# Cutting the last weight loads at other rows, and half as many, twice as wide matmuls, at the end of a two-problem attention kernel

## The chip, the core and the metric

The kernel runs on one core of one Trainium2 chip. The metric is the device time of one execution in microseconds. Lower is better. The profile shows one execution of its own; times of views count from the start of that execution's span.

## The reference

Two attention problems, A and B, are computed with one query token each, and their results are concatenated. Both have 32 query heads, 16 key-value heads, head width 128, a cache of 8192 positions and model width 576, in bfloat16. A looks at the last 2048 positions of its cache alone (`W = min(4096, max(256, Sk // 4))`), B at all.

```python
q = (x @ wq).reshape(B, Sq, Hq, Dh)           # 576 -> 32 * 128
scores = einsum("bhqd,bhkd->bhqk", q, k) * (Dh ** -0.5)
p = softmax(scores, axis=-1)
o = einsum("bhqk,bhkd->bhqd", p, v)
return o.reshape(B, Sq, Hq * Dh) @ wo         # 4096 -> 576
```

The last line is the output projection: a row of 4096 numbers times `wo`, a matrix of 4096 x 576 (4.6 MB). The two results of 576 numbers each stand side by side in the output.

## The kernel before

**Program.** The kernel records every step with `add(engine, ...)` and the names of what it reads and writes; `Program` derives the semaphore waits from these names. Each engine runs its own steps in the order in which they were recorded. There is no scheduler: the order is written out by hand.

**Attention.** The work is done in five groups: group 0 holds the whole of A, groups 1 to 4 hold four key-value heads of B each. Keys and values come in through four slots of SBUF (`slots`, 16384 elements a partition each): two for keys, two for values. In a group TensorE transposes the keys (L464), multiplies them with the queries (L485), and, after the softmax, multiplies the probabilities with the values (L538). VectorE and ScalarE bring the transposed keys from PSUM back to SBUF.

**Loads.** All large loads are issued by SP, on one queue, in the order of the text. A load waits, at its issue, for the work that last read its part of `slots`. After the values of the last group there stand five loads of `wo` (`load_wo`, issued on L391):

- all 32 rows of A's `wo`, into the key slots, as soon as the keys of the last group are transposed;
- 24 rows of B's `wo`, into the rest of the key slots;
- 5 rows of B's, then 2, then 1, into the first value slot, as soon as that was read.

A "row" here is one of the 32 rows that each of the 128 partitions holds: partition p holds the 32 rows of `wo` from 32p on, each of 576 numbers, so a row is 128 x 576 numbers or 144 KB over all partitions.

**Output projection.** `combine` and `o_columns` (L621) leave the attention's result of each problem in `opj`, one column per row of `wo`. `wo_part` then multiplies, row by row: a row's 576 columns are cut into four pieces of 144, and each piece goes through its own strip of 32 columns of TensorE's array, into its own 32 partitions of a PSUM bank (L634). Only the first partition of each strip holds the result; the others are padding. All 32 rows add up in the bank. `wo_part` runs over A's 32 rows first, then over B's in the pieces in which they were loaded, each piece waiting for its own load:

```python
for P in range(2):
    for Q, lo, n, off, res in wo_loads:
        if Q == P:
            wo_part(P, lo, n, off, res)
    finish_out(P)
```

`finish_out` copies the bank to SBUF on VectorE (L640) and lets SP write the 576 numbers out (L646). The program ends when both outputs have landed. A's projection runs while B's loads are still coming in, B's stands at the very end.

Of the kernel before, what the change touches and what calls it, by code (L numbers as in the profile page):

```python
# [4 lines left out]
BF16 = mybir.dt.bfloat16  # L5
# [5 lines left out]
HQ = 32  # L11
HKV = 16
DH = 128
DM = 576
SK = 8192
SCALE = DH ** -0.5
SLOT = 16384
# [1 line left out]
NG = 5  # L19
NKT = 4  # L20
WQ_W = 18432
OUTW = DM // 4


class Op:
# [11 lines left out]
class Program:  # L37
# [15 lines left out]
    def add(self, eng, fn, reads=(), writes=(), dma=None, after=(), tag=None, inc=1, loop=None):  # L53
        op = Op(eng, fn, tuple(reads), tuple(writes), dma, tag, inc if dma is None or inc > 1 else 16, loop)
        deps = []
        for r in op.reads:
            w = self.writer.get(r)
            if w is not None:
                deps.append((w, True))
            if r[0] == "bank":  # L60
                deps += [(o, False) for o in self.readers.get(r, ())]
        for r in after:
            deps += [(o, False) for o in self.readers.get(r, ())]
        for r in op.writes:
            w = self.writer.get(r)
            if w is not None:
                deps.append((w, False))
            deps += [(o, False) for o in self.readers.get(r, ())]
        for r in op.reads:
            self.readers.setdefault(r, []).append(op)  # L70
        for r in op.writes:
            self.writer[r] = op
            self.readers[r] = []
        for o, raw in deps:
            if o is op:
                continue
            if o.dma is None and o.eng == eng and (not raw or eng in ("pe", "sp")):
                continue
            op.deps.append(o)
            o.needed = True  # L80
        op.order = len(self.ops)
        self.ops.append(op)
        return op
# [192 lines left out]
def bass_concat_heads__sliding_block_cached__gqa_block_cached__decode_kernel(  # L276
# [26 lines left out]
    add = prog.add  # L303

    slots = nc.alloc_sbuf_tensor("slots", [128, 4 * SLOT], BF16)
# [21 lines left out]
    acc = nc.alloc_sbuf_tensor("acc", [128, NG, DH], F32)  # L327
    accs = nc.alloc_sbuf_tensor("accs", [128, NG, DH], F32)
    opj = nc.alloc_sbuf_tensor("opj", [128, 2, 64], BF16)
    outsb = nc.alloc_sbuf_tensor("outsb", [128, 2, OUTW], BF16)  # L330
    warm = nc.alloc_sbuf_tensor("warm", [128, 8], F32)

    ktps = [nc.alloc_psum_tensor("ktps%d" % b, [128, 512], F32) for b in range(4)]
# [291 lines left out]
    def load_wo(P, lo, n, off, res):  # L625
        load(slots[:, off:off + n * DM], lambda: wos[P].rearrange("(p j) n -> p (j n)", p=128)[:, lo * DM:(lo + n) * DM],
             res, "wo%d_%d" % (P, lo))

    def wo_part(P, lo, n, off, res):
        def mm(pe):  # L630
            for jj in range(lo, lo + n):
                for j in range(4):
                    o = off + (jj - lo) * DM + j * OUTW
                    ins = pe.matmul(ktps[P][32 * j:32 * j + 32, 0:OUTW], lhsT=opj[:, P, jj:jj + 32],  # L634
                                    rhs=slots[:, o:o + OUTW], start=(jj == 0), stop=(jj == HQ - 1))
            return ins
        add("pe", mm, reads=[("opj", P)] + res, writes=[("bank", P)])

    def finish_out(P):
        add("dve", lambda dve: dve.tensor_copy(outsb[:, P, :], ktps[P][:, 0:OUTW]), reads=[("bank", P)],  # L640
            writes=[("outsb", P)])

        def put(eng):
            src = bass.AP(tensor=outsb, offset=P * OUTW, ap=[[32 * 2 * OUTW, 4], [1, OUTW]])
            dst = out[0, 0:1, P * DM:(P + 1) * DM].rearrange("o (j n) -> (o j) n", j=4)
            return eng.dma_start(dst, src)  # L646
        add("sp", put, reads=[("outsb", P)], writes=[("out", P)], dma="out%d" % P)

# [2 lines left out]
    for P in range(2):  # L651
        off, res = WQ[P]
# [9 lines left out]
        reads=["sameB0"], writes=["sameB"])  # L662
    sums(pickB[:, :, :], pick[:, :, :].rearrange("p r (i c) -> p r c i", i=4), ["pick"], ["pickB"])

    for g in range(NG):
# [30 lines left out]

    wo_loads = [
        (0, 0, 32, 0, [("k", 0), ("k", 1, 0)]),
        (1, 0, 24, WQ_W, [("k", 1, 1)]),
        (1, 24, 5, 2 * SLOT, [("v", 0, 0), ("v", 0, 1)]),  # L700
        (1, 29, 2, 2 * SLOT + 5 * DM, [("w", 0)]),
        (1, 31, 1, 2 * SLOT + 7 * DM, [("w", 1)])]
    for k, (P, lo, n, off, res) in enumerate(wo_loads):
        if res[0][0] == "w":
            wo_loads[k] = (P, lo, n, off, res)
        load_wo(P, lo, n, off, res)
    combine([NG - 1])
    o_columns(1)
# [5 lines that stand above are left out]
    prog.emit()  # L714
    for P in range(2):
        o = prog.writer[("out", P)]
# [28 lines left out]
```

## Time and profile before

| | us |
|---|---|
| median of 5 runs | 248.68 (248.33 to 248.77) |
| profiled execution | 248.85 |
| its span, first to last instruction | 247.2 |
| TensorE busy | 161.8 (65%) |
| DMA engines busy with the large loads' queue | 97.6% of the span |
| read from memory | 102.76 MB, 416 GB/s over the span |
| granted TensorE clock, mean | 0.827 |

PE is TensorE's matmuls, PEld its weight loads (which overlap matmuls), DVE is VectorE, ACT ScalarE, SP the engine that issues the loads; a q behind an engine's name marks its sequencer. L634 is line 634 of the kernel. A group of instructions is written `out<-in`, with its count behind an x. A matmul `ktps<-slots,opj 128*32 128x144` contracts over 128 partitions, with 32 columns of weights (`opj`) and 144 columns streamed (`slots`). Each matmul comes with a weight load. A matmul's duration is longer than the step from one matmul to the next, since they are pipelined. The granted clock is the share of full speed at which TensorE was allowed to run: in these traces 1.00 or 0.50.

### The profile page before, as it was taken

The page shows a single profiled execution, that of the slowest core. Times are in us where ns is not written, and L with a number is a line of the kernel's source. Part 1 is how long each engine was busy: PE and PEld are TensorE (multiplying, and loading weights), DVE is VectorE, ACT ScalarE, POOL GpSimd, SP SyncE. Part 2 cuts the span into 40 slices and gives each one's busy share as a digit, 9 for nine tenths or more (in the row PEclk, how much of TensorE's full clock was granted, in tenths as well). Part 3 has the DMA queues.
Part 4 walks back from the last instruction along what each step waited for, and adds up shares of the span by engine and source line. Part 5 has one row for each costly group of instructions (what it writes and reads, how often), then busy time and mean ns, then how long its engine had stood idle before and what let it go on. Part 6 is the DMA issues. An engine that isn't in the chain of part 4 may idle for free. (4 is left out here: it accounts for less than half of the span.)

```text
span 247.2 us, 5330 instructions
## 1 busy us (share of the span) xinstructions
PE 161.8 (65%) x2348; PEld 116.5 (47%) x2348; DVE 84.9 (34%) x172; ACT 87.4 (35%) x95; POOL 10.7 (4%) x48
## 2 busy tenths in 40 slices
PE   0014639994706999443999380999581799769716
PEld 0001239782306876213887130977340777435516
DVE  0010124654221465240556331355422255524200
ACT  2000016874003786101778200578500387610000
POOL 7400000000000000000000000000000000000000
PEclk9999577999775999795899766599979599965786
DMA  9998999999999999999999999999999999999991
GB/s 358 406 424 372 424 424 422 422 422 419 468 423 419 430 430 435 430 435 445 431 430 430 435 424 430 424 440 424 435 445 430 430 435 435 424 445 412 433 389 67
DMA packets 5929, 102.89 MB, mean 416 GB/s; under 512 B 928, under 2 KB 1056, under 8 KB 1312
## 3 DMA queue, kind: packets, MB, share of 16 engines
q1 hardware_dynamic: 5632, 102.77, 97.6%
q8 instruction: 6, 0.10, 0.2%
q10 hardware_dynamic: 288, 0.00, 0.1%
q14 instruction: 3, 0.02, 0.0%
HBM read 102.76 MB, written 0.00 MB: 416 GB/s over the span
## 5 line engine op out<-in xcount | busy, mean ns | idle before, releaser
L470 ACT ACTIVATE kt<-ktps 128x1024 bf16<-128x1024 bf16 x80 | 78.5, 1021 | 92.1 <-PE ktps L464 92.1
L464 PE MATMUL ktps<-ident,slots 128*128 128x128 bf16 x1280 | 89.2, 236 | 32.7 <-PEq L214 32.7
L464 PEld LDWEIGHTS ktps<-ident,slots 128*128 128x128 bf16 x1280 | 83.4, 107 | 47.9 <-issue 47.9
L473 DVE COPY kt<-ktps 128x1024 bf16<-128x1024 bf16 x80 | 55.3, 692 | 77.0 <-PE ktps L464 77.0
L538 PE MATMUL opsum<-slots,ptm 128*32 128x512 bf16 x320 | 29.4, 525 | 5.9 <-PEq L214 5.9
L485 PE MATMUL sacc<-kt,qst 128*32 128x512 bf16 x320 | 25.4, 393 | 1.9 <-PEq L214 1.9
L425 PE MATMUL opsum<-slots,xpad 128*32 128x512 bf16 x72 | 7.3, 586 | 22.3 <-DVE xpad L416 22.3
L538 PEld LDWEIGHTS opsum<-slots,ptm 128*32 128x32 bf16 x320 | 12.0, 123 | 18.6 <-issue 15.9
L425 PEld LDWEIGHTS opsum<-slots,xpad 128*32 128x32 bf16 x72 | 2.8, 137 | 25.6 <-issue 25.5
L555 DVE SCALAR_TENSOR_TENSOR acc<-opsum,maskV,acc 128x128 f32<-128x128 f32 x28 | 9.8, 351 | 4.5 <-PE opsum L538 3.7
L516 PE MATMUL misc<-ident,psb 128*128 128x128 bf16 x40 | 3.3, 231 | 11.6 <-PEq L214 11.6
L431 ACT ACTIVATE qrow<-opsum 128x512 bf16<-128x512 f32 x2 | 1.2, 597 | 26.4 <-PE opsum L425 26.4
L454 POOL COPY qst<-qcol 128x8 bf16<-128x8 bf16 x20 | 3.1, 190 | 164.5 <-PE sacc L485 152.1
L634 PE MATMUL ktps<-slots,opj 128*32 128x144 bf16 x256 | 6.3, 276 | 5.1 <-DMA slots<-in_B_wo_dram 5.1
L516 PEld LDWEIGHTS misc<-ident,psb 128*128 128x128 bf16 x40 | 2.5, 102 | 14.0 <-issue 14.0
L506 ACT ACTIVATE psb<-sacc,stat 128x1024 bf16<-128x1024 f32 x5 | 5.6, 1113 | 9.5 <-DVE stat L500 9.5
L485 PEld LDWEIGHTS sacc<-kt,qst 128*32 128x32 bf16 x320 | 5.0, 94 | 7.9 <-issue 4.3
L634 PEld LDWEIGHTS ktps<-slots,opj 128*32 128x32 bf16 x256 | 5.8, 122 | 5.3 <-DMA slots<-in_B_wo_dram 5.3
L525 DVE TENSOR_SCALAR ptm<-misc,par 128x512 bf16<-128x512 bf16 x10 | 4.4, 480 | 10.4 <-PE misc L516 10.4
L416 DVE TENSOR_SCALAR xpad<-xtwo,par 128x5 bf16<-128x5 bf16 (+1 forms) x8 | 1.3, 230 | 16.5 <-DMA xtwo<-in_A_x_dram 12.8
L552 DVE TENSOR_SCALAR acc<-opsum,maskV 128x128 f32<-128x128 f32 x4 | 1.4, 351 | 14.1 <-PE opsum L538 14.1
L498 DVE TENSOR_REDUCE stat<-sacc 128x1 f32<-128x512 f32 x5 | 3.5, 691 | 4.5 <-PE sacc L485 4.5
(62 smaller groups left out, 34.5 us busy)
## 6 DMA issues: line engine op xcount, KB each, us to landing
slots<-in_B_k_cache_dram SPq DMA_DIRECT2D x8, 4096.0 KB
slots<-in_B_v_cache_dram SPq DMA_DIRECT2D x8, 4096.0 KB
slots<-in_A_k_cache_dram SPq DMA_DIRECT2D x8, 1024.0 KB
slots<-in_A_v_cache_dram SPq DMA_DIRECT2D x8, 1024.0 KB
slots<-in_A_wq_dram SPq DMA_DIRECT2D x1, 4608.0 KB, 13.8
slots<-in_B_wq_dram SPq DMA_DIRECT2D x1, 4608.0 KB, 24.5
slots<-in_A_wo_dram SPq DMA_DIRECT2D x1, 4608.0 KB, 19.2
slots<-in_B_wo_dram SPq DMA_DIRECT2D x1, 3456.0 KB, 27.0
```

The costliest lines, as they stand in the source:

```text
L425: ins = pe.matmul(opsum[32 * j:32 * j + 32, P * 512:(P + 1) * 512], lhsT=xpad[:, P, u, :], rhs=slots[:, o:o + 512], start=(u == 0), stop=( ...
L464: ins = pe.matmul(ktps_bf[q][:, t * 128:(t + 1) * 128], lhsT=slots[:, o:o + 128], rhs=ident[:, :], start=True, stop=True, is_transpose=True)
L470: add("act", lambda act, q=q, dst=dst: act.activation(dst, ktps_bf[q], ACT.Copy), reads=[("bank", q)], writes=[("kt", u % NKT, q)], tag="e ...
L473: add("dve", lambda dve, q=q, dst=dst: dve.tensor_copy(dst, ktps_bf[q]), reads=[("bank", q)], writes=[("kt", u % NKT, q)], tag="e%d%d" % ( ...
L485: ins = pe.matmul(sacc[32 * j:32 * j + 32, :], lhsT=qst[:, o:o + 32], rhs=rhs, start=(u == 0 and e == 0), stop=True, skip_group_check=True)
L498: add("dve", lambda dve: dve.tensor_reduce(st(C_M + g), sacc[:, :], AX.X, ALU.max), reads=[B_S], writes=[("st", C_M + g)], tag="max")
L506: return act.activation(psb[:, :].rearrange("p (x g) -> p x g", g=2), src, ACT.Exp, bias=st(C_NB + g), scale=SCALE, accum_out=st(C_L + g))
L516: ins = pe.matmul(dst[:, t * 128:(t + 1) * 128], lhsT=psb[:, t * 128:(t + 1) * 128], rhs=ident[:, :], start=True, stop=True, is_transpose= ...
L525: ins = dve.tensor_scalar(to, src, par2[:, e:e + 1], None, ALU.mult)
L538: ins = pe.matmul(opsum[32 * j:32 * j + 32, s * 512:(s + 1) * 512], lhsT=ptm[:, o:o + 32], rhs=v[:, :, b:b + 128], start=(tt == 0), stop=( ...
L555: add("dve", lambda dve, w=w, src=src: dve.scalar_tensor_tensor(dst, src, w, dst, ALU.mult, ALU.add), reads=[B_O[s], "wlast" if last else ...
L634: ins = pe.matmul(ktps[P][32 * j:32 * j + 32, 0:OUTW], lhsT=opj[:, P, jj:jj + 32], rhs=slots[:, o:o + OUTW], start=(jj == 0), stop=(jj == ...
```

## The change

Two things change. A's output projection takes two matmuls of 288 columns per row, through two strips, for four of 144: 64 matmuls for 128, and with their weight loads 128 instructions fewer in TensorE's program. A's copy to SBUF takes 64 partitions x 288 for 128 x 144, and A's output is written as two pieces of 288 numbers for four of 144. B's projection keeps its four matmuls of 144 columns per row. And B's `wo` comes in loads of 21, 7, 3 and 1 rows for 24, 5, 2 and 1; the number of loads, their order and what each waits for at its issue stay, and `wo_part` waits for B's rows in the new pieces. In the changed kernel the matmul's line is 635 for 634, the copy's 643 for 640, the output's 649 for 646.

```diff
-OUTW = DM // 4
+OUTS = [2, 4]
...
-    outsb = nc.alloc_sbuf_tensor("outsb", [128, 2, OUTW], BF16)
+    outsb = nc.alloc_sbuf_tensor("outsb", [128, 2, DM // 2], BF16)
...
             for jj in range(lo, lo + n):
-                for j in range(4):
-                    o = off + (jj - lo) * DM + j * OUTW
-                    ins = pe.matmul(ktps[P][32 * j:32 * j + 32, 0:OUTW], lhsT=opj[:, P, jj:jj + 32],
-                                    rhs=slots[:, o:o + OUTW], start=(jj == 0), stop=(jj == HQ - 1))
+                w = DM // OUTS[P]
+                for j in range(OUTS[P]):
+                    o = off + (jj - lo) * DM + j * w
+                    ins = pe.matmul(ktps[P][32 * j:32 * j + 32, 0:w], lhsT=opj[:, P, jj:jj + 32],
+                                    rhs=slots[:, o:o + w], start=(jj == 0), stop=(jj == HQ - 1))
...
     def finish_out(P):
-        add("dve", lambda dve: dve.tensor_copy(outsb[:, P, :], ktps[P][:, 0:OUTW]), reads=[("bank", P)],
-            writes=[("outsb", P)])
+        n = OUTS[P]
+        add("dve", lambda dve: dve.tensor_copy(outsb[0:32 * n, P, 0:DM // n], ktps[P][0:32 * n, 0:DM // n]),
+            reads=[("bank", P)], writes=[("outsb", P)])
         def put(eng):
-            src = bass.AP(tensor=outsb, offset=P * OUTW, ap=[[32 * 2 * OUTW, 4], [1, OUTW]])
-            dst = out[0, 0:1, P * DM:(P + 1) * DM].rearrange("o (j n) -> (o j) n", j=4)
+            src = bass.AP(tensor=outsb, offset=P * DM // 2, ap=[[32 * DM, n], [1, DM // n]])
+            dst = out[0, 0:1, P * DM:(P + 1) * DM].rearrange("o (j n) -> (o j) n", j=n)
             return eng.dma_start(dst, src)
...
         (0, 0, 32, 0, [("k", 0), ("k", 1, 0)]),
-        (1, 0, 24, WQ_W, [("k", 1, 1)]),
-        (1, 24, 5, 2 * SLOT, [("v", 0, 0), ("v", 0, 1)]),
-        (1, 29, 2, 2 * SLOT + 5 * DM, [("w", 0)]),
-        (1, 31, 1, 2 * SLOT + 7 * DM, [("w", 1)])]
+        (1, 0, 21, WQ_W, [("k", 1, 1)]),
+        (1, 21, 7, 2 * SLOT, [("v", 0, 0), ("v", 0, 1)]),
+        (1, 28, 3, 2 * SLOT + 7 * DM, [("w", 0)]),
+        (1, 31, 1, 2 * SLOT + 10 * DM, [("w", 1)])]
```

More of the change, by code (lines that the diff above doesn't have):

```diff
@@ L698, in bass_concat_heads__sliding_block_cached__gqa_block_cached__decode_kernel @@
         (0, 0, 32, 0, [("k", 0), ("k", 1, 0)]),
-        (1, 0, 24, WQ_W, [("k", 1, 1)]),
-        (1, 24, 5, 2 * SLOT, [("v", 0, 0), ("v", 0, 1)]),
-        (1, 29, 2, 2 * SLOT + 5 * DM, [("w", 0)]),
-        (1, 31, 1, 2 * SLOT + 7 * DM, [("w", 1)])]
-    for k, (P, lo, n, off, res) in enumerate(wo_loads):
-        if res[0][0] == "w":
-            wo_loads[k] = (P, lo, n, off, res)
+        (1, 0, 21, WQ_W, [("k", 1, 1)]),
+        (1, 21, 7, 2 * SLOT, [("v", 0, 0), ("v", 0, 1)]),
+        (1, 28, 3, 2 * SLOT + 7 * DM, [("w", 0)]),
+        (1, 31, 1, 2 * SLOT + 10 * DM, [("w", 1)])]
+    for P, lo, n, off, res in wo_loads:
         load_wo(P, lo, n, off, res)
```

## The prediction

> **What bounds the kernel now.** I read the page's numbers first: the DMA engines are busy 97.6% of the span with the one load queue, TensorE 65%, so up to the last loads the kernel lasts as long as its 102.8 MB. The change touches only what follows the last attention group, so the chain that ended last, the landings and the clock there come next. The end of the chain (start, duration, what):
>
> ```profile
> 214.02 27.05 DMA slots<-in_B_wo_dram
> 241.06 0.04 issue
> 241.11 4.06 PE ktps L634 x112
> 245.17 0.02 issue
> 245.19 0.31 DVE outsb L640
> ```
>
> The span ends at 247.2. TensorE waits until 241.07 for B's first 24 rows, multiplies all 32 rows in one go until 245.14, then come a copy and the output's DMA, which the change leaves alone for B. The question is what holds the 4.06 us. The four loads of B, with the time from issue to landing, and when SP issued three of them (two in the first line, one in the second):
>
> ```profile
> slots<-in_B_wo_dram SPq DMA_DIRECT2D x1, 3456.0 KB, 27.0
> slots<-in_B_wo_dram SPq DMA_DIRECT2D x1, 720.0 KB, 18.2
> slots<-in_B_wo_dram SPq DMA_DIRECT2D x1, 288.0 KB, 18.5
> slots<-in_B_wo_dram SPq DMA_DIRECT2D x1, 144.0 KB, 18.4
> ```
>
> ```profile
> 224.63 0.80 SPq L391 DMA_DIRECT2D slots<-in_B_wo_dram  x2
> 225.48 0.43 SPq L391 DMA_DIRECT2D slots<-in_B_wo_dram  x1
> ```
>
> The 24 rows land at 214.02+27.05 = 241.07, the 5 at 224.63+18.2 = 242.83, the 2 (issued at 225.00, where the first line's second issue begins) at 243.50, the last row at 225.48+18.4 = 243.88. From 241.07 to 243.88 eight rows land in 2.81 us: 0.35 us a row (0.35 over the 5, 0.34 over the 2, 0.38 for the last). All data is there 1.26 us before TensorE ends, so the end is set by TensorE, which starts late and runs slowly. How slowly, the stretches show (us, length, PE busy and count, PEld, DVE, ACT, POOL, then granted clock, DMA share, GB/s):
>
> ```profile
> 231.90:233.70 1.80, 0.12 (x4) 0.13 (x5) 1.40 (x4) 0.00 (x0) 0.00 (x0) 1.00 1.07 461
> 233.70:236.10 2.40, 2.31 (x136) 2.12 (x135) 0.24 (x2) 0.00 (x0) 0.00 (x0) 1.00 0.96 415
> 236.10:238.50 2.40, 0.00 (x0) 0.00 (x0) 0.26 (x1) 0.00 (x0) 0.00 (x0) 1.00 0.94 401
> 238.50:241.10 2.60, 0.00 (x0) 0.00 (x0) 0.00 (x0) 0.00 (x0) 0.00 (x0) 0.51 0.92 369
> 241.10:245.20 4.10, 4.03 (x128) 3.74 (x128) 0.01 (x1) 0.00 (x0) 0.00 (x0) 0.50 0.24 90
> ```
>
> A's 128 matmuls ran at clock 1.00, B's 128 at 0.50: the clock fell at about 238.5, 2.5 us after A's last matmul ended. The timeline gives the rates:
>
> ```profile
> 235.79 0.23 PE L634 MATMUL ktps<-slots,opj 128*32 128x144 bf16 x1
> 236.39 9.68 SPq L646 DMA_DIRECT2D out_dram<-outsb  x2
> 241.11 4.03 PE L634 MATMUL ktps<-slots,opj 128*32 128x144 bf16 x128 [5.09 <-DMA slots<-in_B_wo_dram]
> ```
>
> A's matmuls start from 233.73 to 235.79: 2.06 us over 127 steps, 16.2 ns each, 65 ns for a row of four. B's last matmul takes 0.32 us, so its 127 steps fill 4.03-0.32 = 3.71 us: 29.2 ns each, 117 ns a row.
>
> **The change, part by part.**
>
> *The first load, 21 rows for 24.* The bytes ahead of the last of those rows shrink by three rows, and the queue never empties, so it lands between 241.07 (no gain) and 241.07-3×0.35 = 240.02. I take 240.02: the three later landings kept the pace of 0.35 us a row whatever the size of the load. TensorE then starts at 240.06 (0.04 after landing, as before).
>
> *The later loads, 7, 3 and 1 rows for 5, 2 and 1.* After them 28, 31 and 32 rows are there; 31 and 32 are the old cuts, so these land at 243.50 and 243.88 as before, and 28 rows at 242.83-0.35 = 242.48. The number of loads and SP's issues and waits stay; the second load waits for the same V slot, the two small ones for nothing.
>
> *A's matmuls, 64 of 288 columns for 128 of 144.* Each row streams the same 576 columns through two 32-column strips of the array, not four. No row of this trace shows two strips beside each other. If issue alone set the pace, 64×16.2 ns = 1.0 us; if nothing ran beside anything, four times 65 ns a row, 8.3 us. I take twice the four-strip price, 130 ns a row, because the columns in each strip double: 4.2 us, so A ends at 233.73+4.2+0.2 = 238.1 for 236.0. That is covered by the wait for B's load until 240.06; the cover ends when A takes over 6.3 us.
>
> The Trainium skill speaks against this part: "TensorE: Matmul & The Clock Gate", Part 3 (packing small matmuls), says that matmuls in different strips run at once and that more strips give more. Its isolated gap of N/2.4+2.5 ns would be 122.5 ns for 288 columns; 64 in a row, none overlapped, would be an estimated 7.8 us, with the end then near the late case below.
>
> *B's matmuls* are unchanged, but each load's rows now wait for their own landing. At half clock: 21 rows from 240.06 to 242.52, 7 rows to 243.34, 3 rows from 243.54 to 243.89, the last from 243.92; its four matmuls end 3×0.029+0.32 = 0.41 later, at 244.33, for 245.14: 0.81 saved. At full clock: 241.43, then 7 rows from 242.52 to 242.98, 3 from 243.54 to 243.74, the last from 243.92 to 243.92+3×0.016+0.23 = 244.20: 0.94 saved. So the clock decides little here; the last landing decides.
>
> Which clock? A's later end shortens the idle time from 5.1 us to 240.06-238.1 = 2.0 us. An idle stretch of about 1.6 us (232.0 to 233.6) kept 1.00, one of 2.5 us lost it: 2.0 lies between, nearer the one that kept it, so full clock is likelier.
>
> The same page, Part 1 (the clock gate), says that the gate falls to half after an idle window of about 3.4 us, free-running against the kernel. Here it fell after 2.5 us of idleness, so a bare rule of 3.4 us of gap isn't what this trace shows; by the page the new gap would keep the clock, and the sum would be the 0.94 above.
>
> If A alone is late (8.3 us, end at 242.3), B follows at full clock: 32 rows × 65 ns = 2.1, plus 0.2 for the last, end 244.65, still 0.5 saved.
>
> *A's copy and output.* The copy takes 64x288 for 128x144, between its old 0.31 and 0.62 us, from 238.1; the issue of A's output moves from 236.39 to about 238.6. Behind it on SP stands only B's output at 245.2 at the earliest today, 244.3 then, over 5 us later. Cost nothing; the wait for the copy that ends last on SP stays B's.
>
> *Code.* TensorE's program loses 64 matmuls and 64 weight loads. The code queue moves:
>
> ```profile
> q8 instruction: 6, 0.10, 0.2%
> ```
>
> about 16.4 KB apiece; one of the six lies after 240 us. At 416/16 = 26 GB/s an engine, one costs its DMA engine 0.63 us. If a fetch goes away from the engine that ends last, up to 0.63 is gained; if one moves onto it, 0.63 is lost. I take 0: the four landings keep their even pace, so neither late fetch seems to sit on that engine.
>
> **Sum.** Against the profiled execution (248.85 us for a span of 247.2, 1.65 around it): 0.81 to 0.94 off the end of TensorE, after which nothing changes (copy 0.31, output 1.7). I take 0.85: 248.0. The median of the runs, 248.68, is 0.17 under the profiled execution, so 247.83 there; I state 247.9, since runs in which the clock returned before B's end have a little less to gain.
>
> **The rivals.**
>
> 1. *The landing doesn't move.* If 21 rows land when 24 did (241.07) and the clock is half, B ends at 245.14: 248.7. The even 0.35 us a row speaks against it, and at full clock the end would still be bounded by 243.88. Chance 0.08.
> 2. *A code fetch falls on the engine that lands last.* The last landing goes from 243.88 to 244.5, the gain to 0.2: 248.5. For: the program's shift by 128 instructions moves the fetch among B's matmuls. Against: the last fetch came too late to matter before, and moves towards the program's end. Chance 0.10.
> 3. *Slower: the clock falls during A.* If two strips count as too little work, A runs at half clock: a row takes 2×117 = 234 ns if pairs overlap, 4×117 = 468 if nothing does; say 300, nearer the pairs. A then ends at 233.73+32×0.3+0.3 = 243.6, B from there at half clock at 243.6+31×0.117+0.41 = 247.65, 2.5 later: 251.2. It decides once A ends after 241.05 with B at half clock (an A row of over 220 ns). Against: B's 32 rows at half clock brought the clock back to 1.00 by 245.5, and A's work is longer than today's. Chance 0.06.
>
> **The numbers.** Forecast 0.76, by itself 247.6 to 248.2 (0.81 to 0.94 with the runs' own scatter of 0.4). The range of 247.4 to 248.5 takes in a vanished code fetch below and rival 2 above; rivals 1 and 3 stay outside. A measurement of this kernel tells about 0.2% (0.5 us) from no change: under 248.2 is faster, over 249.2 slower. Faster: 0.76 and a share of rival 2, 0.80; within: the rest of 2 and 1, 0.14; slower: 0.06.
>
> **What would show it.** Right: B's first matmul near 240.1, A's last near 238, TensorE idle twice or more among B's rows before landings, the last row's matmuls right behind a landing near 243.9, the chain ending in the load of one row instead of 24. Wrong steps would show as: a first matmul still at 241.1 (landing), A's matmuls running past 240 (strips), B's matmuls back to back to 245 (start or clock), a last landing past 244.3 (code or load shape). The forecast as a whole fails if TensorE's last matmul ends after 244.7.

## The result, and the profile after

| | before | after |
|---|---|---|
| median, us | 248.54 (49 runs, 247.66 to 249.24) | 247.88 (28 runs, 247.34 to 248.81) |
| profiled execution, us | 248.85 | 247.49 |
| its span, us | 247.2 | 245.8 |
| code queue | 6 transfers | 5 transfers |

The ratio is 0.9977, with a 95% interval of 0.9969 to 0.9985: 0.57 us (0.37 to 0.77) off 248.54. The kernel became faster: the interval leaves out no change, though the gain is a quarter of a per cent. The later sets of runs gave 1.12 and 0.80 us (below).

The end of the chain in the profiled execution after the change (start, duration, what):

```profile
224.08 18.99 DMA slots<-in_B_wo_dram
243.07 0.04 issue
243.12 0.37 PE ktps L635 x12
243.49 0.00 issue
243.49 0.28 PE ktps L635 x4
243.76 0.02 issue
243.79 0.31 DVE outsb L643
```

Before, the chain's last transfer was the 24-row load and 4.06 us of matmuls stood behind it. Now its last transfer is a small load, and what stands behind it is the last three rows and the last row. The landings and the issues by SP:

```profile
slots<-in_B_wo_dram SPq DMA_DIRECT2D x1, 3024.0 KB, 26.9
slots<-in_B_wo_dram SPq DMA_DIRECT2D x1, 1008.0 KB, 18.4
slots<-in_B_wo_dram SPq DMA_DIRECT2D x1, 432.0 KB, 19.0
slots<-in_B_wo_dram SPq DMA_DIRECT2D x1, 144.0 KB, 18.9
```

```profile
212.73 12.26 SPq L391 DMA_DIRECT2D slots<-in_B_wo_dram  x4
223.71 0.80 SPq L391 DMA_DIRECT2D slots<-in_B_wo_dram  x2
224.56 0.43 SPq L391 DMA_DIRECT2D slots<-in_B_wo_dram  x1
```

21 rows land at 212.73+26.9 = 239.63, 28 at 223.71+18.4 = 242.11, 31 at 224.08+19.0 = 243.08, all 32 at 224.56+18.9 = 243.46. TensorE's side, in the timeline (the bracket is the idle time before and what ended it):

```profile
239.64 1.50 PE L635 MATMUL ktps<-slots,opj 128*32 128x144 bf16 x84 [0.95 <-DMA slots<-in_B_wo_dram]
242.17 0.62 PE L635 MATMUL ktps<-slots,opj 128*32 128x144 bf16 x28 [1.03 <-DMA slots<-in_B_wo_dram]
243.12 0.62 PE L635 MATMUL ktps<-slots,opj 128*32 128x144 bf16 x16 [0.33 <-DMA slots<-in_B_wo_dram]
243.49 0.10 PEld L635 LDWEIGHTS ktps<-slots,opj 128*32 128x32 bf16 x4 [0.19 <-DMA slots<-in_B_wo_dram]
```

TensorE now waits for every one of the four landings, and ends at 243.74, 0.28 us after the last one. Before, it ended 1.26 us after it (245.14 to 243.88). The stretches, with clock, DMA share and GB/s at the end of each row, show at what clock:

```profile
232.90:236.30 3.40, 3.40 (x38) 2.24 (x38) 0.19 (x1) 0.00 (x0) 0.00 (x0) 0.50 1.01 434
236.30:238.70 2.40, 2.39 (x38) 1.69 (x34) 0.00 (x0) 0.00 (x0) 0.00 (x0) 0.99 0.86 366
238.70:239.60 0.90, 0.00 (x0) 0.00 (x0) 0.45 (x1) 0.00 (x0) 0.00 (x0) 1.00 0.92 384
239.60:241.20 1.60, 1.50 (x84) 1.31 (x84) 0.00 (x0) 0.00 (x0) 0.00 (x0) 1.00 0.98 385
241.20:243.80 2.60, 1.24 (x44) 0.72 (x44) 0.01 (x1) 0.00 (x0) 0.00 (x0) 1.00 0.27 100
```

A's 64 matmuls ran at 0.50 for 3.4 us, and the clock came back to 1.00 before they were done; B ran at 1.00 throughout. The code queue, which brings TensorE's program (a transfer on it is called a code fetch below), had five transfers:

```profile
q8 instruction: 5, 0.08, 0.1%
```

### The profile page after: what moved, and what is told of

Same layout as the page of the kernel before. It is cut to its first block, busy times and chain, and to the rows that moved or that the text cites. A ratio compares the mean times of both kernels' runs of the same rounds, so it can differ in the third digit from the quotient of the medians.

```text
span 245.8 us, 5202 instructions
## 1 busy us (share of the span) xinstructions
PE 164.7 (67%) x2284; PEld 115.1 (47%) x2284; DVE 85.0 (35%) x172; ACT 87.1 (35%) x95; POOL 10.8 (4%) x48
## 5 line engine op out<-in xcount | busy, mean ns | idle before, releaser
L464 PE MATMUL ktps<-ident,slots 128*128 128x128 bf16 x1280 | 86.5, 232 | 32.4 <-PEq L214 32.4
L464 PEld LDWEIGHTS ktps<-ident,slots 128*128 128x128 bf16 x1280 | 80.7, 105 | 47.7 <-issue 47.7
L538 PE MATMUL opsum<-slots,ptm 128*32 128x512 bf16 x320 | 31.0, 548 | 5.4 <-PEq L214 5.4
L425 PE MATMUL opsum<-slots,xpad 128*32 128x512 bf16 x72 | 8.1, 630 | 21.5 <-DVE xpad L416 21.5
L516 PE MATMUL misc<-ident,psb 128*128 128x128 bf16 x40 | 4.4, 276 | 11.6 <-PEq L214 11.6
L635 PE MATMUL ktps<-slots,opj 128*32 128x144 bf16 (+1 forms) x192 | 8.5, 270 | 2.3 <-DMA slots<-in_B_wo_dram 2.3
L516 PEld LDWEIGHTS misc<-ident,psb 128*128 128x128 bf16 x40 | 3.3, 122 | 14.0 <-issue 14.0
## 6 DMA issues: line engine op xcount, KB each, us to landing
slots<-in_B_wo_dram SPq DMA_DIRECT2D x1, 3024.0 KB, 26.9
```

The source lines that it names most:

```text
L425: ins = pe.matmul(opsum[32 * j:32 * j + 32, P * 512:(P + 1) * 512], lhsT=xpad[:, P, u, :], rhs=slots[:, o:o + 512], start=(u == 0), stop=( ...
L464: ins = pe.matmul(ktps_bf[q][:, t * 128:(t + 1) * 128], lhsT=slots[:, o:o + 128], rhs=ident[:, :], start=True, stop=True, is_transpose=True)
L516: ins = pe.matmul(dst[:, t * 128:(t + 1) * 128], lhsT=psb[:, t * 128:(t + 1) * 128], rhs=ident[:, :], start=True, stop=True, is_transpose= ...
L538: ins = pe.matmul(opsum[32 * j:32 * j + 32, s * 512:(s + 1) * 512], lhsT=ptm[:, o:o + 32], rhs=v[:, :, b:b + 128], start=(tt == 0), stop=( ...
L635: ins = pe.matmul(ktps[P][32 * j:32 * j + 32, 0:w], lhsT=opj[:, P, jj:jj + 32], rhs=slots[:, o:o + w], start=(jj == 0), stop=(jj == HQ - 1))
```

## The experiments

Theory L: the last landing is a floor for TensorE's end, and B's matmuls reach it either by starting earlier (the cut) or by running at full clock (what fills the idle time before B), so one of the two is enough. Against it stood: only the clock counts (C), only the cut counts (S), the two gains add up, or the shorter program is what helps.

All times below are against the kernel before, run beside it on the same chip. For the gain in us the ratio is applied to the median of the kernel before in the same set of runs. The sets e1 to e4, e5 to e8 and e9 to e12 each ran on a chip of their own.

| run | ratio, interval | us | last landing | TensorE ends | between |
|---|---|---|---|---|---|
| before, first profile | | | 243.88 | 245.14 | 1.26 |
| e5 before, again | 1.0000 (0.9986 to 1.0014) | 0.0 | 244.01 | 245.25 | 1.24 |
| e1 cut only | 0.9980 (0.9963 to 0.9997) | -0.50 | 244.04 | 244.34 | 0.30 |
| e9 cut only, again | 0.9966 (0.9948 to 0.9985) | -0.85 | 243.79 | 244.20 | 0.41 |
| e2 strips only | 0.9968 (0.9955 to 0.9981) | -0.80 | 243.89 | 244.22 | 0.33 |
| e10 strips only, again | 0.9975 (0.9950 to 1.0001) | -0.62 | 243.67 | 244.03 | 0.36 |
| e6 filler of 48 matmuls | 0.9964 (0.9946 to 0.9983) | -0.89 | 244.19 | 244.51 | 0.32 |
| e4 whole change | 0.9955 (0.9942 to 0.9968) | -1.12 | 243.43 | 243.69 | 0.26 |
| e11 whole change, again | 0.9968 (0.9948 to 0.9988) | -0.80 | 243.56 | 243.83 | 0.27 |
| e3 filler of 128 matmuls | 1.0024 (1.0007 to 1.0041) | +0.60 | 243.56 | 245.64 | 2.08 |
| e7 last row first | 1.0128 (1.0108 to 1.0147) | +3.18 | 243.83 | 247.90 | 4.07 |
| e8 pad of 64 | 0.9994 (0.9979 to 1.0009) | -0.15 | 244.13 | 244.42 | 0.29 |
| e12 pad of 256 | 1.0022 (0.9996 to 1.0047) | +0.55 | 244.82 | 245.11 | 0.29 |

The last three columns come from one profiled execution of each: the last load's issue and its time to landing, and the end of the last matmul. The views give the time to landing to 0.1 us, so the last column is good to about 0.05. They show two things apart: the landing, which wanders from execution to execution, and what TensorE adds to it.

**The cut alone (e1, e9).**

```diff
-OUTS = [2, 4]
+OUTS = [4, 4]          # the changed kernel, A back in four strips
```

> Only the loads of 21, 7, 3 and 1 rows; A keeps four strips of 144 columns and the program its length. Theory L (the last landing bounds the end; an earlier start and a full clock are each enough to get there): B starts about 1.0 us before where it starts with 24 rows, still at clock 0.50, and its last row starts within 0.1 us of the last landing; TensorE ends about 0.4 us after that landing, the time is 0.5 to 0.8 us under the kernel before. Rival C (only the clock counts, the cut does nothing): same as before within 0.2 us. Rival S (only the cut counts): the whole gain of the change, the same time as the changed kernel within 0.1 us.

> The cut alone once more (loads of 21, 7, 3 and 1 rows, A in four strips), beside the other part and the whole change on one chip, for narrower intervals. Theory L (each part is enough): 0.6 to 1.0 us under the kernel before, within 0.3 us of the whole change; TensorE ends 0.3 to 0.4 us after the last landing. Theory of separate gains: 0.3 to 0.5 us under before and as far above the whole change.

In e1 B's matmuls start at 240.25 and run at half clock nearly to the end, as in the kernel before:

```profile
240.20:243.70 3.50, 3.45 (x112) 3.26 (x112) 0.00 (x0) 0.00 (x0) 0.00 (x0) 0.51 0.56 221
243.70:244.40 0.70, 0.64 (x20) 0.29 (x16) 0.01 (x1) 0.00 (x0) 0.00 (x0) 1.00 0.00 0
```

Yet they end 0.30 us behind the last landing, where the kernel before needs 1.24 to 1.26: an earlier start alone reaches the floor (the last rows ran at 1.00 here). So rival C is wrong. In e9 the last rows ran at 0.50 and the end came 0.41 after the landing, the price that the prediction had for half clock.

**The strips alone (e2, e10).**

```diff
-        (1, 0, 21, WQ_W, [("k", 1, 1)]),
-        (1, 21, 7, 2 * SLOT, [("v", 0, 0), ("v", 0, 1)]),
-        (1, 28, 3, 2 * SLOT + 7 * DM, [("w", 0)]),
-        (1, 31, 1, 2 * SLOT + 10 * DM, [("w", 1)])]
+        (1, 0, 24, WQ_W, [("k", 1, 1)]),
+        (1, 24, 5, 2 * SLOT, [("v", 0, 0), ("v", 0, 1)]),
+        (1, 29, 2, 2 * SLOT + 5 * DM, [("w", 0)]),
+        (1, 31, 1, 2 * SLOT + 7 * DM, [("w", 1)])]
```

> Only A's 64 matmuls of 288 columns in two strips (128 instructions fewer); B's loads stay at 24, 5, 2 and 1 rows. Theory L: B starts when 24 rows have landed (about 241), at clock 1.00, does these 24 rows in 1.6 us and waits for each later landing; TensorE ends 0.3 us after the last landing, 0.6 to 0.9 us under the kernel before, and within 0.2 us of the changed kernel. Rival C: the same. Rival S: no gain, TensorE busy without a break from 241 on.

> A in two strips alone once more (loads of 24, 5, 2 and 1 rows). Theory L: 0.6 to 1.0 us under before, within 0.3 us of the whole change. Theory of separate gains: as for the cut alone, and both differences add up to that of the whole change.

In e2 B starts at 241.14, as late as in the kernel before, but at full clock:

```profile
238.30:241.10 2.80, 0.00 (x0) 0.00 (x0) 0.45 (x1) 0.00 (x0) 0.00 (x0) 1.00 0.93 372
241.10:242.40 1.30, 1.26 (x80) 1.26 (x84) 0.00 (x0) 0.00 (x0) 0.00 (x0) 0.99 0.48 182
242.40:244.30 1.90, 1.82 (x60) 1.24 (x48) 0.03 (x1) 0.00 (x0) 0.00 (x0) 0.50 0.13 38
```

80 of the 128 matmuls have begun by 242.4, when the clock falls; B then goes on without a break, which the expectation had otherwise, and the end comes 0.33 us behind the landing. So rival S is wrong too.

That the clock holds for 2.8 us of idleness here, but fell 2.5 us after A in the kernel before, shows that the length of the gap alone doesn't decide. The clock records show more: in all fourteen profiles the clock changes only at points that lie whole multiples of 3.41 us apart, and these points fall at other times in each execution. In the kernel before, TensorE was busy for 0.89 us of the stretch from 235.12 to 238.53, and the clock fell at its end. In e2 the idle time is spread over two such stretches: 235.54 to 238.95 (busy 2.73 us, clock kept) and 238.95 to 242.37 (busy 1.23 us, clock lost). So how long B keeps the full clock depends in part on where these points happen to fall. How much work a stretch needs isn't settled: in e10 1.37 us kept the clock in one stretch and lost it in the next.

**The whole change beside its parts (e4, e11).** The kernel is the changed one.

> The changed kernel itself, on the same chip as the parts. Theory L: 0.6 to 0.9 us under the kernel before, no more than 0.2 us under the better of the two parts, and far from the sum of both. Theory of two separate gains: the sum of what the two parts give.

> The whole change once more, beside its parts. Theory L: 0.7 to 1.0 us under before and no more than 0.3 us under the better part. Theory of separate gains: the sum of the parts.

e4 missed its expectation: 0.32 us under the better part rather than 0.2, and not far from the sum of the two (1.30). In the second set, on another chip, the cut gave 0.85, the strips 0.62 and both 0.80, where two separate gains would have given 1.47. The intervals are too wide for the times alone to decide (e11's goes from 0.30 to 1.29 us). The profiles say more: the six kernels end 0.26 to 0.41 us after their landings, against 1.24 to 1.26 before. Either part alone takes away nearly all of that distance, and the other adds at most 0.15 us to it.

The landing is another matter. In the three profiles of the changed kernel the last landing came at 243.43 to 243.56, in the four of its parts at 243.67 to 244.04. The difference is there already when A's `wo` lands (232.4 to 232.5 for 232.7 to 233.0), before the first instruction in which these kernels differ has run. So it is no work of the cut or of the strips as theory L has them; whether these three executions happened to land early, or something else about the program makes them, stays open.

**Fillers in place of the strips (e3, e6).** A's strips stay at four, the loads at 24, 5, 2 and 1; matmuls whose result isn't read go between A and B.

```diff
+            for jj in range(HQ):                 # e3: A's 128 matmuls of 144 columns again, into bank 2
...
+            for t in range(12):                  # e6: 4 * 12 matmuls of 512 columns, into bank 2
...
```

> The kernel before, with A's 128 matmuls in four strips done a second time into an unused PSUM bank (the result isn't read), so that TensorE is idle for about 3 us less before B; loads of 24, 5, 2 and 1 rows; the program is 256 instructions longer. Theory L with the clock as the means: B starts at clock 1.00 or comes to it early, and the time is 0.4 to 0.9 us under the kernel before, though nothing useful was taken away. If it is the shorter program (fewer code fetches) that makes strips faster: no gain here, or 0.2 to 0.6 us slower. Rival S: no gain.

> The kernel before, with 48 matmuls of 512 columns in four strips into an unused PSUM bank between A and B (96 instructions for the 256 of the first filler; the result isn't read). A's own part, the loads and B stay as before. Theory L with the clock as means: no break for code, B starts with its 24 rows' landing at clock 1.00 or comes to it before its end, waits for the later landings, and TensorE ends 0.3 to 0.4 us after the last one: 0.5 to 0.9 us under the kernel before. Rival (the strips help by something other than TensorE's work in the gap, fewer instructions for example): no gain.

e3 went the other way, and the chain says why:

```profile
237.24 0.88 PE ktps L644 x56
238.12 2.74 issue
240.86 2.34 PE ktps L644 x69
243.20 2.45 PE ktps L634 x128
```

After 59 of the filler's 128 matmuls TensorE stood still for 2.74 us with no semaphore to wait for. In just that stretch, 238.2 to 240.8, the code queue moved one block:

```profile
q8 instruction: 1, 0.02, 2.6%
```

By its record this transfer ended at 239.51, and the matmuls went on at 240.86, 1.35 us later. In e12 (below) the same happens among the small matmuls at the start: TensorE stood from 9.69 to 12.46, again with no semaphore to wait for, a block came in from 10.17 to 11.11, and matmuls went on 1.35 us after it. So TensorE had most likely run out of fetched code both times, though no record names that wait. B's first matmul in e3 then came at 242.88, 2.1 us after its 24 rows had landed (213.04+27.7 = 240.74). So e3 tells nothing of the clock, and its loss of 0.60, which the expectation gave for a program's length as the cause, is explained by this stop. e6 fills the time with 96 instructions instead of 256, and there the filler runs without a break and the gain is there:

```profile
236.50:239.20 2.70, 2.70 (x60) 1.10 (x48) 0.31 (x1) 0.00 (x0) 0.00 (x0) 1.00 0.90 377
239.20:241.40 2.20, 0.04 (x7) 0.01 (x4) 0.00 (x0) 0.00 (x0) 0.00 (x0) 1.00 0.90 359
241.40:244.50 3.10, 3.10 (x128) 2.33 (x128) 0.00 (x0) 0.00 (x0) 0.00 (x0) 0.71 0.29 111
```

0.89 us faster, with work added and none taken away, and with B starting at clock 1.00. What helps is the work in the time before B, by way of the clock, and not a shorter program. The two strips fill that time because they are slow, not because they are fewer.

**The kernel before against itself (e5).** No edit.

> The kernel before against itself, as a control and for a second look at its end. All theories: the same within 0.3 us, which shows the scatter of the comparison. Theory L: TensorE ends 0.8 to 1.3 us after the last landing, since all or nearly all of B's rows run at clock 0.50; the spans of single executions differ by about 1 us, because the last landing itself comes at different times. If the last landing is found within 0.4 us of TensorE's end here, the theory that a late and slow TensorE was what the change removed is wrong.

The second profile finds the same end: `x128` from 241.22 at clock 0.50, done 1.24 us after the landing.

```profile
241.20:245.30 4.10, 4.03 (x128) 3.74 (x128) 0.00 (x0) 0.00 (x0) 0.00 (x0) 0.50 0.24 87
```

**The last row first (e7).**

```diff
-        for Q, lo, n, off, res in wo_loads:
+        for Q, lo, n, off, res in wo_loads[::-1]:
...
```

The marks of the first and the last row of a sum (`start`, `stop`) move with the order.

> The changed kernel, with B's pieces multiplied in the reverse order: the row that is loaded last comes first, so TensorE waits for the last landing and then does all 32 rows. Theory L (the last landing is a floor, and each row left behind it costs its price): with the clock fallen to 0.50 in a gap of about 5 us, 32 rows of 117 ns and a last matmul, 4.1 us after the landing, 3.8 us over the changed kernel; at clock 1.00 2.3 us after it, 2.0 over. If the landing is not the floor, less than 1 us over it.

TensorE waits for the last landing and then does all of B at 0.50; it ends 4.07 us after the landing, where 4.1 was expected, and the kernel is 3.18 us slower than before. The landing is a floor, and a row left behind it costs 117 ns at half clock (4.03 us less 0.32 for the last matmul, over 127 steps, times four).

**The program's old length (e8), and longer (e12).** 64 or 256 matmuls of 8 columns at the start of TensorE's program, where it has nothing to do until about 17 us (e8's take 1.9 us).

```diff
...
+            for t in range(64):                  # e12: 256
+                ins = pe.matmul(sacc[0:32, 0:8], lhsT=ident[:, 0:32], rhs=ident[:, 0:8], start=True, stop=True)
...
```

> The changed kernel with 64 matmuls of 8 columns (128 instructions with their weight loads) at the start of TensorE's program, into a bank that is overwritten later, while TensorE waits for the first weights: the program is as long as the kernel before's again and every code fetch falls 128 instructions earlier in what follows. Theory L: the same as the changed kernel within 0.2 us, six code fetches in place of five. Rival (the shorter program is what brings the gain): 0.3 us or more slower than the changed kernel, or TensorE standing still for code among its last matmuls.

> The changed kernel with 256 small matmuls (512 instructions, two more code fetches of 16 KB than the pad of 64) at the start of TensorE's program, where it waits for the first weights anyway. Theory F (a code fetch puts back the one DMA engine that carries it, that engine stays behind to the end, and the last landing is that of the engine furthest behind): the spread between the first and the last engine to finish a load steps up at the time of each fetch that hits an engine already behind, stays after that, and the last landing comes 0.3 to 1.0 us later than in the changed kernel; TensorE still ends 0.3 us after it. Rival (the pad of 64 cost time by something in TensorE's own program): the last landing as in the changed kernel, the time lost between it and the end.

e8 missed: nearly all of the gain is gone. That is what the rival, the shorter program, had forecast; but e6 and e9, whose programs are no shorter than the kernel before's, have the whole gain. TensorE loses nothing at the end, either: it ends 0.29 us after the landing in e8 and e12. It is the landing that comes later, at 244.13 and 244.82 for 243.43 to 243.56 in the changed kernel. In e12 that is more than the 0.3 to 1.0 us expected, and its loss of 0.55 against the kernel before is at the edge of what its interval tells from nothing.

The packets' records suggest what moves the landing. Each load ends with sixteen marks there, one for each DMA engine, and has landed when the last is in. This is the spread between the first mark and the last, in us, for loads that finish at about these times (us), with the code fetches up to then:

```
                fetches begin at              spread at   13    25    37    43    51    66    232
before          39.0 48.6 58.3 71.3                       0.8   0.9   0.9   1.7   2.3   2.4   2.2
e5 before       39.2 47.4 57.8 71.6                       0.9   1.1   1.0   1.9   1.9   2.5   2.6
after           38.9 47.5 57.4 70.1                       0.7   0.9   0.8   1.7   1.9   2.0   2.1
e11 after       39.4 48.5 58.2 70.3                       0.8   1.1   1.2   1.7   2.1   2.2   2.2
e8 pad of 64    22.5 46.2 56.1 65.6                       0.6   1.4   1.3   1.3   2.3   2.5   2.7
e12 pad of 256  10.2 17.1 40.5 48.5 56.1 71.5             1.8   1.8   2.7   1.9   1.9   2.8   2.9
```

The spread steps up at some of the fetches, and what it is at 66 us it still is, within 0.2, at 232. In e8 the step at 39 is gone, and steps at 22.5 and 46.2 stand in its place; in e12 the first comes at 10. (In e12 it also falls once, from 2.7 to 1.9 around 40 us.) The landing goes with the spread: over all fourteen profiles a spread of 2.1 to 2.3 us at 232 comes with last landings at 243.43 to 243.88, one of 2.5 to 2.6 with 243.67 to 244.04, one of 2.7 with 244.13 and 244.19, and one of 2.9 with 244.82.

This speaks for theory F: a fetch puts one engine back, and the engine furthest behind sets the last landing. It doesn't prove it. The spread of e8 (2.5 and 2.7) is nearly that of e5 (2.5 and 2.6), which has no pad, and its landing lies within the 243.43 to 244.19 of the kernels without one. In e12 the first engine, too, ends the load of A's `wo` 0.6 us later than in e11 (230.4 for 229.8), and where that comes from stays open. No run took one of the early fetches away.

No run was clearly faster than the changed kernel, and e6, e9 and e2 come as close to it as the intervals can tell. Given its landing, TensorE's end is 0.26 to 0.28 us from the floor.

## Why the prediction was right

The time was forecast at 247.9 and measured at 247.88, and faster was forecast with 0.80. The mechanism held: TensorE's end went from 1.26 us behind the last landing to 0.28. That the time was met to 0.02 us is luck. The forecast took 0.78 us off a median of 248.68; the result's runs put that median at 248.54, and the gain at 0.57 (later sets at 1.12 and 0.80). By its steps:

- **The first landing.** Right. It moved with its rows: 11 rows land from 239.63 to 243.46, 0.35 us a row, and e1 has it without any other change.
- **The later landings.** Right in kind: the pace stays, whatever the sizes (0.35, 0.32 and 0.38 us a row over the 7, the 3 and the 1). Rival 1, landings that don't move, is out.
- **A's two strips.** The price of 130 ns a row was 6% high: in e11, at full clock, the 64 matmuls of 288 columns start from 233.42 to 237.23, 3.81 us over 31 steps from pair to pair, 123 ns each. The second matmul of a pair starts 3 to 4 ns after the first and the next pair 119 ns later, so two strips do run beside each other. But the step had A at clock 1.00, as it was in the profile before, and that isn't fixed: in all later profiles but e11 A began at 0.50, also with four strips (e1, e5, e6). A ended at 238.7 for the 238.1 forecast, and the gap before B was 0.95 us for 2.0. A had cover until 239.6. What the step did not see is that the strips are worth something by themselves: without the cut they reach the floor as well (e2, e10).
- **The clock under B.** The likelier case came: B at 1.00 in the three profiles of the changed kernel. The working by two ends, 0.81 and 0.94 saved, held: TensorE ends 0.28 us after the landing at full clock (0.32 worked out) and 0.41 at half (e9; 0.45 worked out).
- **The rule on the gate.** The case came, but not for the reason given. The step went by the length of the gap, and a gap of 2.5 us lost the clock where one of 2.8 us (e2) kept it. The Trainium skill, "TensorE: Matmul & The Clock Gate", Part 1, says that the window is free-running; the points 3.41 us apart that fall at other times in each execution agree with that, and a limit on the gap by itself can't give both. Part 3 of that page, on matmuls in different strips running at once, agrees with the pairs above. The prediction read it as speaking against the price, but at 65 ns for four strips and 123 ns for two it speaks for it. The 7.8 us for matmuls that don't overlap did not come: e11's A took 4.1.
- **Code.** Taken as nothing, and for the change itself that held. By the packets' records, the last packet of B's `wo` ends 11.0 to 11.1 us after the last packet of A's `wo`, in the two profiles of the kernel before and the three of the changed one, though the late code fetches lie at 238.0 to 243.0 in the one and at 238.8 to 239.9 in the other. Rival 2 did not occur. What the step didn't ask is whether code fetches matter long before: by theory F they set up the spread that the last landing inherits.
- **The sum.** 0.85 was taken. The profiled executions lose 0.98 between landing and end (1.26 to 0.28), the result's medians 0.57, later ones 1.12 and 0.80. The term that was too firm is the landing: taken as 243.88 for both, it came between 243.43 and 244.19 in executions whose programs are alike up to A's matmuls. The spans of the two profiles of the kernel before (247.2 and 247.3) are 1.3 to 1.6 us above those of the changed kernel (245.7 to 245.9), of which 0.3 to 0.6 is the landing; they also lie above the 246.8 median of the 20 executions beside e1 to e4. Whether other executions of the kernel before end closer to their landing was not seen, and stays open.
- **Rival 3**, the clock falling during A, happened in half: A ran at 0.50 for 3.4 us, but the clock was back at 1.00 at 236.3 with A still running, so two strips were work enough for it, and A ended long before the 241.05 from which the rival would have decided.

## What to carry to other kernels

When the last work waits for a stream of loads, find the last landing first, then ask how far behind it the last instruction ends; that distance is all that a better cut, a faster clock or fewer instructions can win, and whichever reaches it first leaves little to the others (here 0.15 us at most). Slow work in front of a wait can be worth more than fast work, because it can keep the matmul clock up for what comes after the wait (here 0.62 to 0.89 us in e2, e10 and e6). And look at the scatter of executions before believing a difference of 0.2%: here the landing alone wanders by 0.8 us between kernels whose programs are alike up to A's matmuls.

## What the runs showed of the hardware that was not expected

- TensorE can stop among matmuls that wait for no semaphore: 2.74 us at 238.12 in e3 and 2.77 us at 9.69 in e12. Both times one block of 16 KB moved on the code queue meanwhile, and the matmuls went on 1.35 us after its transfer had ended. With 96 filler instructions for e3's 256 in the same place (e6) there was no such stop.
- The clock changes on a grid of 3.41 us (all fourteen profiles), whose place differs from execution to execution, so an idle time of 2.5 us lost the full clock and one of 2.8 us kept it.
- The lag of a DMA engine is kept: the spread that has formed by 66 us (2.0 to 2.8) stands at 232 us within 0.2, and it grew in steps at some of TensorE's code fetches. With 128 instructions added at the start of the program, where TensorE is idle, the last landing came 0.6 to 0.7 us later in the profiled execution than in the three of the changed kernel, and the gain of 0.57 to 1.12 us shrank to 0.15.
